# Linear attention plus a routed MLP: eight row numbers loaded at once, and four short runs of the middle stage set in another order

## The chip, the core and the metric

The kernel runs on one core of a Trainium2 chip. The metric is the device time of one execution in microseconds (us), lower is better; times below are in us unless marked ns.

The core's engines work at the same time, each through its own instructions in order, and wait for each other on semaphores: TensorE (PE; PEld are its weight loads) multiplies matrices into PSUM, which has eight banks; VectorE (DVE), ScalarE (ACT) and GpSimd (POOL) work on elements; SyncE (SP) here only issues DMAs.

## The reference, cut

```python
xn = layernorm(x)                                   # x: 2048 x 640, bf16
# A: linear attention, 32 heads of 20
q, k, v = split(xn @ wqkv);  pq, pk = phi(q), phi(k)   # phi(t) = t + 1 or exp(t)
kv, z = pk^T v, sum(pk)                             # per head
A = ((pq kv) / (pq z)) @ wo
# B: eight rows through an MLP
r = xn @ w_r;  idx = the 8 largest of r
y = (silu(xn[idx] @ w_gate) * (xn[idx] @ w_up)) @ w_down * sigmoid(r[idx])
out = x + A + xn + scatter(y at idx)
```

## The kernel before

The 2048 rows are 16 tiles of 128, the 640 columns five chunks of 128. The order on each engine is that of the code (`manual_schedule`); nothing is moved by a scheduler. Semaphore waits are derived from what each instruction reads and writes.

**First stage**, to about 62.8 us: norm, turning (xnT), k, phi(k) into `pk`, q into `pqT`, and G = xn^T pk, which with wv gives kv without v being computed. Columns 0 to 511 of G gather in PSUM banks 0 to 4 (`g_mm`).

**Middle stage**, 62.8 to 82.4 us, where the change lies:

- `grest_mm` (L283) makes G's last 128 columns: 64 matmuls for the first four chunks, 16 for the fifth, all reading `pk`.
- VectorE finds the eight rows (L543 to L560). GpSimd reads the eight numbers one after the other with `value_load` (L565) and copies one column of xnT for each into `xsT` (L566).
- `den_mm` (L581) makes pq z for the first half of the rows, `den_act` (L592, L593) its reciprocal on ScalarE, `spread_mm` (L598) spreads that over the partitions into banks 0 to 3, `spread_copy` (L607) copies it into `spw`, and `scale_by` (L611) multiplies `pqT` by it, a chunk at a time.
- `kv_mm` (L621) makes kv for six groups of heads, `kv_mask` (L633, L640) masks it; `m_mm` (L652) multiplies each group by wo, `m_out` (L664 on ScalarE or L666 on VectorE) copies the result and stores it by SyncE (L667) into M_sb.
- `gu_mm` (L673) makes gate and up from xsT. ScalarE takes Exp, Ln and Exp of gate (L725 to L730, tiles e1 and sg), VectorE two products (L733, L734, tile hm), TensorE turns hm (L741), VectorE copies it (L743, tile hT), and the down product (L749) gives y, which VectorE scales (L756) and GpSimd adds into DRAM (L759); from there x is loaded again (L765).
- `q_mm` (L247) with `q_act` (L259, L260) and `q_phi` (L266) does the remaining q units 13 to 19, a unit being 512 rows of one chunk.

`den_mm`, `gu_mm` and the down product use TensorE as four tiles 32 columns wide, the spread as four tiles of 32 rows; all others use it whole.

Two tiles share memory: `late` is opened under the tag of `pk`, so it has pk's bytes, and whoever writes it waits for pk's readers. M_sb, e1, sg, hm and hT are parts of it:

```python
    late = big.tile([P, T * D], BF16, tag="pk", name="late")
    M_sb = late[:, 0 : KC * D].rearrange("p (k d) -> p k d", k=KC)
    e1 = late[:, o0 : o0 + 2 * FJ].bitcast(F32)
```

**Last stage**, from 82.4 us: per tile of rows ten matmuls pqT x M (L790), VectorE adds x + xn (L800), and the tile is stored. The denominators of the second half run between them.

Of the kernel before, what the change touches and what calls it, by code (L numbers as in the profile page):

```python
# [8 lines left out]
P = 128  # L9
S = 2048  # L10
D = 640
# [3 lines left out]
T = S // P  # L15
# [30 lines left out]
def kernel(  # L46
# [28 lines left out]
    def sb(shape, dt, name, pool=None, tag=None):  # L75
        return (pool or big).tile(shape, dt, tag=tag or name, name=name)
# [34 lines left out]
    candm = sb([P, 2, T, C], BF16, "candm")  # L111
    M_nat5 = sb([GB, D], BF16, "M_nat5")
    spw = sb([P, 2, 4, 256], BF16, "spw")

    ps = psum.tile([P, 8, 512], F32, tag="ps", name="ps")
    xxd = dram.tile([4 * S + P, YW], BF16, tag="xxd", name="xxd")
# [260 lines left out]
    def const_piece(i):  # L377
        if i == 0:
            nc.gpsimd.memset(headg[:], 1.0)
            nc.gpsimd.affine_select(  # L380
                out=headg[:], in_=headg[:], compare_op=ALU.is_ge, fill=0.0, base=0,
                pattern=[[-4, H]], channel_multiplier=1,
            )
            nc.gpsimd.affine_select(
                out=headg[:], in_=headg[:], compare_op=ALU.is_ge, fill=0.0, base=3,
                pattern=[[4, H]], channel_multiplier=-1,
            )
            nc.gpsimd.memset(ones_bf[:], 1.0)
            nc.gpsimd.memset(eps6[:], 1e-6)
            nc.gpsimd.memset(xsT[:], 0.0)  # L390
        elif i == 1:
            nc.gpsimd.memset(maskkv[:], 1.0)
            nc.gpsimd.affine_select(
                out=maskkv[:], in_=maskkv[:], compare_op=ALU.is_ge, fill=0.0, base=0,
                pattern=[[-DH, HG], [0, DH]], channel_multiplier=1,
            )
            nc.gpsimd.affine_select(
                out=maskkv[:], in_=maskkv[:], compare_op=ALU.is_ge, fill=0.0, base=DH - 1,
                pattern=[[DH, HG], [0, DH]], channel_multiplier=-1,
            )  # L400
        elif i == 4:
            nc.gpsimd.memset(ones_r[:], 1.0)
            nc.gpsimd.memset(candm[:], 0.0)
            nc.gpsimd.memset(kvT[:, NG - 1, 0 : W0], 0.0)
            nc.gpsimd.memset(diag[:], 0.0)
            nc.gpsimd.affine_select(
                out=diag[:], in_=diag[:], compare_op=ALU.not_equal, fill=1.0, base=0,
                pattern=[[-1, T]], channel_multiplier=1,
            )
            nc.gpsimd.memset(oh8[:], 0.0)  # L410
            for j in range(4):
                nc.gpsimd.affine_select(
                    out=oh8[:], in_=oh8[:], compare_op=ALU.not_equal, fill=1.0,
                    base=-32 * j, pattern=[[-1, C]], channel_multiplier=1,
                )
        elif i == 5:
            nc.gpsimd.iota(itmp[:], pattern=[[1, P]], base=0, channel_multiplier=0)
            nc.gpsimd.tensor_copy(iot[:], itmp[:])
            nc.gpsimd.iota(
                itmp[:].rearrange("p (t c) -> p t c", c=C), pattern=[[P, T], [0, C]], base=0,  # L420
                channel_multiplier=0,
            )
            nc.gpsimd.tensor_copy(
                tileoff[:], itmp[:].rearrange("p (t c) -> p t c", c=C)
            )
        elif i == 6:
            nc.gpsimd.iota(itmp[:, 0:1], pattern=[[0, 1]], base=4 * S, channel_multiplier=1)
            nc.gpsimd.tensor_copy(yoff[:, 1:2], itmp[:, 0:1])
            nc.gpsimd.memset(yoff[:, 0:1], 0.0)
            for j in range(4):  # L430
                sl = slice(32 * j, 32 * j + C)
                nc.gpsimd.memset(yoff[sl, 0:1], 4.0)
                nc.gpsimd.memset(yoff[sl, 1:2], float(j))
# [97 lines left out]
    )  # L531
    for c in range(KC):
        nc.scalar.copy(GT[:, c, 0:512], ps[:, c, :])
    for t in range(9):
        grest_mm(t, 0, 4, 7)

    allc = sb([P, P], F32, "allc")
    gv = sb([P, C], F32, "gv")
    posu = sb([P, C], U32, "posu")
    junk = sb([P, P], F32, "junk")  # L540
    pcol = sb([P, 4], F32, "pcol")
    idxw = sb([P, 2], U32, "idxw")
    nc.vector.max(gv[:], ps[:, 5, 0:P])  # L543
    nc.vector.max_index(posu[:], gv[:], ps[:, 5, 0:P])
    nc.vector.tensor_tensor(
# [4 lines left out]

    nc.vector.scalar_tensor_tensor(
        out=junk[:, 0:C], in0=posu[:], scalar=1.0, in1=oh8[:], op0=ALU.mult, op1=ALU.mult,
        accum_out=pcol[:, 0:1],
    )
    nc.vector.scalar_tensor_tensor(
        out=junk[:], in0=iot[:], scalar=pcol[:, 0:1], in1=allc[:], op0=ALU.is_equal,
        op1=ALU.mult, accum_out=pcol[:, 1:2],
    )
    nc.vector.tensor_copy(idxw[:, 0:1], pcol[:, 1:2])
    nc.vector.tensor_scalar(  # L560
        out=idxw[:, 1:2], in0=pcol[:, 1:2], scalar1=yoff[:, 0:1], scalar2=yoff[:, 1:2],
        op0=ALU.mult, op1=ALU.add,
    )
    for i in range(C):
        tok = nc.gpsimd.value_load(idxw[i : i + 1, 0:1], min_val=0, max_val=S - 1)  # L565
        nc.gpsimd.tensor_copy(xsT[:, :, i : i + 1], xnT[:, :, bass.ds(tok, 1)])  # L566

    nc.vector.transpose(zT[:], zs[:])
# [8 lines left out]
    def den_mm(h, b):  # L577
        for kc in range(KC):
            for j in range(4):
                o = h * HALF + 256 * j  # L580
                nc.tensor.matmul(  # L581
                    ps[32 * j : 32 * j + 32, b, 0:256],
                    lhsT=zm[:, kc, :],
                    rhs=pqT[:, kc, o : o + 256],
                    start=(kc == 0), stop=(kc == KC - 1),
                    tile_position=(0, 32 * j),
                )
# [15 lines left out]
                tile_position=(32 * j, 0),  # L603
            )

    def spread_copy(h):
        nc.scalar.copy(spw[:, h, :, :], ps[:, 0:4, 0:256])  # L607

    def scale_by(h, m):
        dst = pqT[:, m, h * HALF : (h + 1) * HALF].rearrange("p (j f) -> p j f", j=4)  # L610
        nc.vector.tensor_tensor(out=dst, in0=dst, in1=spw[:, h, :, :], op=ALU.mult)  # L611

    den_mm(0, 6)
    den_act(0, 6)


    def kv_mm(g0, g1, bank):
# [72 lines left out]
    def q_unit(u, b):  # L690
        q_mm(u, b)
        q_act(u, b)
# [7 lines left out]
    with nc.allow_low_precision(reason="gate is bf16 as in the reference"):  # L700
        nc.vector.reciprocal(gbf[:], gcol[:, 2:3])
    nc.vector.tensor_copy(gcol[:, 3:4], gbf[:])
    kv_mm(0, 4, 4)
    kv_mask(0, 4, 4)
    for t in range(9, 11):
        grest_mm(t, 0, 4, 7)
    spread_mm(0)
    spread_copy(0)
    for t in range(11, T):
        grest_mm(t, 0, 4, 7)  # L710
    nc.scalar.copy(GT[:, 0:4, 512:D], ps[:, 7, :].rearrange("p (c f) -> p c f", c=4))
    m_mm(0, 4)
    m_out(0, 4)
    m_mm(1, 0)
    m_out(1, 0, True)
    m_mm(2, 2)
    m_out(2, 2)
    for t in range(T):
        grest_mm(t, 4, 5, 6)
    nc.vector.tensor_copy(GT[:, 4, 512:D], ps[:, 6, 0:P])  # L720
    m_mm(3, 4)
    m_out(3, 4, True)
    scale_by(0, 0)
    gu_mm(wg_sb, 7)
    nc.scalar.activation(e1, ps[:, 7, 0:FJ], AF.Exp, scale=-1.0)  # L725
    gu_mm(wu_sb, 0)
    kv_mm(4, 6, 6)
    scale_by(0, 1)
    nc.scalar.activation(e1, e1, AF.Ln, bias=1.0)
    nc.scalar.activation(sg, e1, AF.Exp, scale=-1.0)  # L730
    kv_mask(4, 5, 6)
    kv_mask5(6)
    nc.vector.tensor_tensor(out=hm, in0=ps[:, 7, 0:FJ], in1=sg, op=ALU.mult)  # L733
    nc.vector.tensor_tensor(out=hm, in0=hm, in1=ps[:, 0, 0:FJ], op=ALU.mult)  # L734
    q_unit(13, 1)
    m_mm(4, 2)
    m_out(4, 2, True)
    m_mm(5, 4)
    m_out(5, 4, True)
    for j in range(3):  # L740
        nc.tensor.transpose(psb(7)[:, j * P : (j + 1) * P], hm[:, j * P : (j + 1) * P], ident[:])  # L741
    q_mm(14, 6, 0, 3)
    nc.vector.tensor_copy(hT, psb(7)[:, 0:FJ].rearrange("p (b c) -> p b c", b=3))  # L743
    q_phi(13)
    scale_by(0, 2)
    for fc in range(FC):
        j, b = fc // 3, fc % 3
        for i in range(4):
            nc.tensor.matmul(  # L749
                ps[32 * i : 32 * i + 32, 0, 0:YW],  # L750
                lhsT=hT[:, b, 32 * j : 32 * j + 32],
                rhs=wd_sb[:, fc, i * YW : (i + 1) * YW],
                start=(fc == 0), stop=(fc == FC - 1),
                tile_position=(0, 32 * i),
            )
    nc.vector.tensor_scalar(  # L756
        out=y_sb[:], in0=ps[:, 0, 0:YW], scalar1=gcol[:, 3:4], scalar2=None, op0=ALU.mult
    )
    nc.gpsimd.indirect_dma_start(  # L759
        xxd[:], bass.IndirectOffsetOnAxis(ap=idxw[:, 1:2], axis=0), y_sb[:], None,  # L760
        compute_op=ALU.add,
    )

    def reload(t0, t1):
        nc.sync.dma_start(x_sb[:, t0:t1, :], xxd_v[:, t0:t1, :])  # L765
# [1 line left out]
    for t0, t1 in ((0, 1), (1, 2), (2, 4), (4, 6), (6, 8)):  # L767
        reload(t0, t1)

    q_mm(14, 6, 3)  # L770
    q_act(14, 6)
    scale_by(0, 3)
    q_phi(14)
    q_unit(15, 2)
    scale_by(0, 4)
    q_phi(15)
    q_unit(16, 3)
    q_phi(16)
    q_unit(17, 1)
    q_phi(17)  # L780
    q_unit(18, 2)
    q_phi(18)
    q_unit(19, 0)
    q_phi(19)


# [81 lines left out]
```

## Time and profile before

| | |
|---|---|
| median of 3 runs | 110.23 us (110.07 to 110.24) |
| the profiled execution's own time | 110.28 us |
| its span, first to last instruction | 108.6 us |
| TensorE busy | 103.9 us, 96% of the span |
| VectorE, ScalarE, GpSimd busy | 82.8, 58.0, 28.9 us |
| granted TensorE clock, mean | 1.000 |

The profile is of one execution. Its timeline rows give the start in us from the span's start, the length, the engine, the source line, the operation, out<-in and a count, and in brackets the engine's idle time before and what ended it. A row that merges several instructions goes from the first's start to the last's end; a matmul's end is modelled and lies after the start of the next, so that the pace of matmuls is read from start to start. POOLq and SPq are the sequencers of GpSimd and SyncE, which load registers and issue DMAs.

### The profile page before, as it was taken

How to read it: one execution, taken by the hardware profiler on the slowest of the kernel's cores; microseconds unless marked ns; L12 is line 12 of the kernel's file. 1: busy time of each engine (PE TensorE's matmuls, PEld its weight loads, DVE VectorE, ACT ScalarE, POOL GpSimd, SP SyncE). 2: the span in 40 equal slices, each digit the busy share in tenths (PEclk: the TensorE clock that was granted, in tenths of full speed). 3: DMA queues.
4: the chain of work that ended last, by engine and by line, in shares of the span. 5: the costliest groups of instructions: out<-in, count | busy, mean ns of one | idle time of the engine just before them, and what ended most of it. 6: DMA issues, size and time to landing. Idle time of an engine off the chain costs nothing.

```text
span 108.6 us, 2418 instructions
## 1 busy us (share of the span) xinstructions
PE 103.9 (96%) x881; PEld 66.0 (61%) x881; DVE 82.8 (76%) x183; ACT 58.0 (53%) x122; POOL 28.9 (27%) x84
## 2 busy tenths in 40 slices
PE   4999999999999999999999999999999999999980
PEld 1376565566555665566556688965656577777760
DVE  0778998989888888988788983558786669966670
ACT  1548846855686558755785574776798330000000
POOL 7402033567744987630000003300420000000000
PEclk9999999999999999999999999999999999999999
DMA  3998961263999999999954799425227928993333
GB/s 97 303 298 265 366 245 25 40 122 60 277 218 191 228 358 189 305 374 300 367 217 166 221 293 374 150 76 157 75 16 203 339 75 231 285 324 132 127 120 114
DMA packets 23096, 22.59 MB, mean 208 GB/s; under 512 B 8796, under 2 KB 21804, under 8 KB 23084
## 3 DMA queue, kind: packets, MB, share of 16 engines
q1 hardware_dynamic: 21106, 20.37, 65.1%
q10 hardware_dynamic: 1834, 2.02, 5.5%
q0 software_dynamic: 144, 0.04, 0.6%
q8 instruction: 7, 0.11, 0.4%
q14 instruction: 5, 0.04, 0.1%
HBM read 14.52 MB, written 5.28 MB: 182 GB/s over the span
## 4 chain that ended last, share of the span: by engine, by line
PE 94%; DVE 2%; POOL 0%; issue 0%; DVEq 0%; POOLq 0%
PE ps L213 20%; PE ps L247 20%; PE ps L790 19%; PE ps L274 16%; PE ps L283 4%; PE ps L294 4%; PE ps L621 2%; PE ps L673 2%; PE ps L195 2%; PE ps L652 2%; DVE xn L800 1%; PE ps L581 1%; PE ps L503 1%; PE ps L749 1%; POOL GT L134 0%; PE ps L598 0%
## 5 line engine op out<-in xcount | busy, mean ns | idle before, releaser
L213 PE MATMUL ps<-wk_sb,xnT 128*128 128x320 bf16 (+1 forms) x160 | 24.6, 300 | 0.2 <-DVE xnT L205 0.2
L247 PE MATMUL ps<-xnT,wq_sb 128*128 128x512 bf16 x100 | 24.2, 379 | 0.0
L790 PE MATMUL ps<-late,pqT 128*128 128x320 bf16 (+2 forms) x165 | 22.3, 295 | 0.0
L213 PEld LDWEIGHTS <-xnT 128*128 128x128 bf16 x160 | 15.3, 98 | 8.4 <-DVE xnT L205 0.5
L274 PE MATMUL ps<-pk,xn 128*128 128x512 bf16 x80 | 19.8, 379 | 0.0
L790 PEld LDWEIGHTS <-pqT 128*128 128x128 bf16 x165 | 15.8, 98 | 6.3 <-issue 0.2
L229 ACT ACTIVATE ek<-ps 128x640 bf16<-128x640 f32 x16 | 11.3, 703 | 15.1 <-PE ps L213 15.1
L800 DVE TENSOR_TENSOR xn<-ps,x_sb 128x640 bf16<-128x640 f32 (+3 forms) x18 | 13.2, 748 | 5.5 <-PE ps L790 5.5
L247 PEld LDWEIGHTS <-wq_sb 128*128 128x128 bf16 x100 | 11.5, 118 | 7.7
L266 DVE SCALAR_TENSOR_TENSOR pqT<-eq,rq 128x512 bf16<-128x512 bf16 x20 | 13.8, 688 | 2.8 <-ACT rq L260 2.8
L236 DVE SCALAR_TENSOR_TENSOR pk<-ek,rk 128x640 bf16<-128x640 bf16 x16 | 12.9, 805 | 1.7 <-ACT rk L230 1.6
L259 ACT ACTIVATE eq<-ps 128x512 bf16<-128x512 f32 x20 | 12.3, 617 | 2.7 <-PE ps L247 2.7
L274 PEld LDWEIGHTS <-xn 128*128 128x128 bf16 x80 | 7.7, 98 | 8.4
L260 ACT ACTIVATE rq<-ps 128x512 bf16<-128x512 f32 x20 | 12.3, 616 | 0.0
L230 ACT ACTIVATE rk<-ps 128x640 bf16<-128x640 f32 x16 | 11.2, 700 | 0.0
L171 POOL TENSOR_TENSOR rs<-mv,half 128x1 f32<-128x1 f32 x13 | 5.8, 449 | 18.1 <-DVE mv L169 18.1
L174 POOL TENSOR_TENSOR rs<-rs,half 128x1 f32<-128x1 f32 x13 | 10.0, 767 | 1.0
L165 DVE BATCH_NORM_STATS2 st<-x_sb 128x6 f32<-128x320 bf16 x16 | 7.6, 478 | 3.2 <-DMA x_sb<-in_A_x_dram 3.2
L183 DVE TENSOR_SCALAR xn<-x_sb,mv,rs 128x640 bf16<-128x640 bf16 x16 | 7.2, 449 | 3.4 <-POOL rs L174 3.3
L168 DVE BATCH_NORM_STATS2 st<-x_sb 128x6 f32<-128x320 bf16 x16 | 7.6, 477 | 0.0
L566 POOL COPY xsT<-xnT 128x5 bf16 x8 | 1.6, 206 | 21.7 <-DVE junk L694 18.3
L189 DVE TENSOR_TENSOR x_sb<-x_sb,xn 128x640 bf16<-128x640 bf16 x16 | 6.9, 476 | 0.0
(123 smaller groups left out, 94.2 us busy)
## 6 DMA issues: line engine op xcount, KB each, us to landing
x_sb<-in_A_x_dram SPq DMA_DIRECT2D x6, 320.0 KB, 8.2
wg_sb<-in_B_w_gate_dram SPq DMA_DIRECT2D x5, 384.0 KB, 4.2
wu_sb<-in_B_w_up_dram SPq DMA_DIRECT2D x5, 384.0 KB, 5.6
wd_sb<-in_B_w_down_dram SPq DMA_DIRECT2D x3, 640.0 KB, 8.3
xxd<-x_sb SPq DMA_DIRECT2D x2, 640.0 KB
out_dram<-xn SPq DMA_DIRECT2D x8, 160.0 KB, 1.8
x_sb<-xxd SPq DMA_DIRECT2D x2, 640.0 KB, 4.9
out_dram<-xn ACTq DMA_DIRECT2D x7, 160.0 KB, 3.2
```

The lines of the kernel that those rows point to most:

```text
L174: nc.gpsimd.tensor_tensor(out=rs[:, 1:2], in0=rs[:, 0:1], in1=half[:, 1:2], op=ALU.pow)
L213: nc.tensor.matmul(ps[:, b + h, 0:w], lhsT=xnT[:, kc, t * P : (t + 1) * P], rhs=wk_sb[:, kc, h * HW : h * HW + w], start=(kc == 0), stop=( ...
L229: nc.scalar.activation(e[:], ps[:, b : b + 2, 0:HW], AF.Exp)
L230: nc.scalar.activation(r[:], ps[:, b : b + 2, 0:HW], AF.Relu)
L236: nc.vector.scalar_tensor_tensor(out=pk[:, t, :].rearrange("p (b f) -> p b f", b=2), in0=e[:], scalar=1.0, in1=r[:], op0=ALU.min, op1=ALU.add,
L247: nc.tensor.matmul(ps[:, b, :], lhsT=wq_sb[:, kc, :].rearrange("p (f m) -> p m f", m=KC)[:, m, :], rhs=xnT[:, kc, tb * TBLK : (tb + 1) * T ...
L259: nc.scalar.activation(e[:], ps[:, b, :], AF.Exp)
L260: nc.scalar.activation(r[:], ps[:, b, :], AF.Relu)
L266: nc.vector.scalar_tensor_tensor(out=pqT[:, m, tb * TBLK : (tb + 1) * TBLK], in0=e[:], scalar=1.0, in1=r[:], op0=ALU.min, op1=ALU.add,)
L274: nc.tensor.matmul(ps[:, c, :], lhsT=xn[:, t, c * P : (c + 1) * P], rhs=pk[:, t, 0:512], start=(t == 0), stop=(t == T - 1),)
L790: nc.tensor.matmul(ps[:, b, 0 : c1 - c0], lhsT=pqT[:, kc, t * P : (t + 1) * P], rhs=M_sb[:, kc, c0:c1], start=(kc == 0), stop=(kc == KC - 1),)
L800: nc.vector.tensor_tensor(out=xn[:, t, c0:c1].rearrange("p (b f) -> p b f", f=w), in0=ps[:, b : b + n, 0:w], in1=x_sb[:, t, c0:c1].rearran ...
```

## The change

**Row numbers.** VectorE gathers the eight numbers in one column of `pcol`, turns that 32x32 block into a row (`prow`), takes the minimum with 2047 into `idxr`, and GpSimd loads all eight registers with one instruction, without a check of bounds for each. The eight copies follow.

**Order of the middle stage.** All 64 matmuls of `grest_mm` for the first four chunks come first, then kv of four groups, then den, gate, up and the spread without others between them, then the 16 of the fifth chunk. q unit 13, M of groups 0 and 1, the turning of hm, kv of the last two groups, M of group 2, the down product, and M of groups 3 to 5 follow, then q units 14 to 19, with a `scale_by` after each `q_phi`. The spread's copy is split: banks 2 and 3 go to VectorE, banks 0 and 1 to ScalarE. Banks are given out anew. No matmul is added or taken away.

```diff
+    pcol = sb([P, 32], F32, "pcol")
...
+            nc.gpsimd.memset(pcol[:], 0.0)
...
-    for t in range(9):
+    for t in range(T):
         grest_mm(t, 0, 4, 7)
...
-    nc.vector.tensor_copy(idxw[:, 0:1], pcol[:, 1:2])
+    nc.vector.transpose(prow[:], pcol[0:32, :])
     nc.vector.tensor_scalar(
+        out=idxr[:], in0=prow[0:1, 0:C], scalar1=float(S - 1), scalar2=None, op0=ALU.min
+    )
...
-    for i in range(C):
-        tok = nc.gpsimd.value_load(idxw[i : i + 1, 0:1], min_val=0, max_val=S - 1)
+    _, toks = nc.values_load_multi_w_load_instructions(
+        idxr[0:1, 0:C], engines=[mybir.EngineType.Pool], min_val=0, max_val=S - 1,
...
+    for i, tok in enumerate(toks):
         nc.gpsimd.tensor_copy(xsT[:, :, i : i + 1], xnT[:, :, bass.ds(tok, 1)])
...
-    den_mm(0, 6)
-    den_act(0, 6)
...
-    kv_mm(0, 4, 4)
-    kv_mask(0, 4, 4)
-    for t in range(9, 11):
-        grest_mm(t, 0, 4, 7)
-    spread_mm(0)
-    spread_copy(0)
-    for t in range(11, T):
-        grest_mm(t, 0, 4, 7)
-    nc.scalar.copy(GT[:, 0:4, 512:D], ps[:, 7, :].rearrange("p (c f) -> p c f", c=4))
-    m_mm(0, 4)
-    m_out(0, 4)
+    kv_mm(0, 4, 5)
+    nc.scalar.copy(GT[:, 0:4, 512:D], ps[:, 7, :].rearrange("p (c f) -> p c f", c=4))
+    kv_mask(0, 4, 5)
+    den_mm(0, 6)
+    den_act(0, 6)
+    gu_mm(wg_sb, 4)
+    nc.scalar.activation(e1, ps[:, 4, 0:FJ], AF.Exp, scale=-1.0)
+    gu_mm(wu_sb, 5)
+    nc.scalar.activation(e1, e1, AF.Ln, bias=1.0)
+    nc.scalar.activation(sg, e1, AF.Exp, scale=-1.0)
+    spread_mm(0)
+    spread_copy(0, 2, 4, False)
+    spread_copy(0, 0, 2)
+    for t in range(T):
+        grest_mm(t, 4, 5, 7)
+    nc.vector.tensor_copy(GT[:, 4, 512:D], ps[:, 7, 0:P])
+    nc.vector.tensor_tensor(out=hm, in0=ps[:, 4, 0:FJ], in1=sg, op=ALU.mult)
+    nc.vector.tensor_tensor(out=hm, in0=hm, in1=ps[:, 5, 0:FJ], op=ALU.mult)
+    q_unit(13, 6)
+    m_mm(0, 2)
+    m_out(0, 2)
     m_mm(1, 0)
     m_out(1, 0, True)
...
+    kv_mm(4, 6, 7)
+    kv_mask(4, 5, 7)
+    kv_mask5(7)
     m_mm(2, 2)
-    m_out(2, 2)
-    for t in range(T):
-        grest_mm(t, 4, 5, 6)
-    nc.vector.tensor_copy(GT[:, 4, 512:D], ps[:, 6, 0:P])
-    m_mm(3, 4)
-    m_out(3, 4, True)
-    scale_by(0, 0)
-    gu_mm(wg_sb, 7)
...
+    m_out(2, 2, True)
...
+    m_mm(3, 0)
+    m_out(3, 0, True)
+    m_mm(4, 2)
+    m_out(4, 2)
+    m_mm(5, 6)
+    m_out(5, 6, True)
+    q_unit(14, 4)
+    q_phi(13)
...
+    scale_by(0, 0)
+    q_unit(15, 5)
+    q_phi(14)
+    scale_by(0, 1)
...
```

ScalarE's instructions in the middle stage before, from the copies of G on (`ld` and `rd` are the reciprocals, `late` the three activations on gate, `M_nat` are groups of M):

```order
L533 CAST GT<-ps 128x512 x5
L592 ACTIVATE ld_1138<-ps,eps_100 128x256
L593 ACTIVATE rd_1139<-ld_1138 128x256
L698 ACTIVATE gcol<-gcol 128x1
L607 CAST spw<-ps 128x1024
L711 CAST GT<-ps 128x4x128
L664 CAST M_nat<-ps 120x640 x2
L725 ACTIVATE late<-ps 128x384
L729 ACTIVATE late<-late 128x384
L730 ACTIVATE late<-late 128x384
```

The same place of the changed kernel, with its own line numbers:

```order
L535 CAST GT<-ps 128x512 x5
L709 ACTIVATE gcol<-gcol 128x1
L715 CAST GT<-ps 128x4x128
L602 ACTIVATE ld_1147<-ps,eps_100 128x256
L603 ACTIVATE rd_1148<-ld_1147 128x256
L720 ACTIVATE late<-ps 128x384
L722 ACTIVATE late<-late 128x384
L723 ACTIVATE late<-late 128x384
L619 CAST spw<-ps 128x512
L260 ACTIVATE eq_1224<-ps 128x512
L261 ACTIVATE rq_1225<-ps 128x512
L675 CAST M_nat<-ps 120x640 x3
```

The three activations on gate stood behind the spread's copy and two groups of M; now they stand ahead of the spread's copy (half as long), of q unit 13 and of all of M.

VectorE behind the mask of the first four groups, before:

```order
L633 TENSOR_TENSOR kvT<-ps,maskkv 120x480
L666 CAST M_nat<-ps 120x640 x2
L720 CAST GT<-ps 128x128
L611 TENSOR_TENSOR pqT<-pqT,spw 128x1024 x2
L633 TENSOR_TENSOR kvT<-ps,maskkv 120x120
L640 TENSOR_TENSOR kvT<-ps,maskkv 120x40
L733 TENSOR_TENSOR late<-ps,late 128x384
L734 TENSOR_TENSOR late<-late,ps 128x384
L743 COPY late<-ps 128x384
```

and in the changed kernel:

```order
L644 TENSOR_TENSOR kvT<-ps,maskkv 120x480
L621 CAST spw<-ps 128x512
L729 CAST GT<-ps 128x128
L730 TENSOR_TENSOR late<-ps,late 128x384
L731 TENSOR_TENSOR late<-late,ps 128x384
L677 CAST M_nat<-ps 120x640
L739 COPY late<-ps 128x384
L644 TENSOR_TENSOR kvT<-ps,maskkv 120x120
L651 TENSOR_TENSOR kvT<-ps,maskkv 120x40
```

The two products of hm moved ahead of every copy of M and of every scaling of pqT, and one copy of M stands between them and the copy of hT.

GpSimd at the row numbers, before, the first two of eight turns (ISA rows compute on registers):

```order
L565 TENSOR_LOAD idxw
L565 ISA x2
L566 ISA
L566 COPY xsT<-xnT 128x5
L565 TENSOR_LOAD idxw
```

and in the changed kernel, the load and the first two of eight copies:

```order
L571 TENSOR_LOAD idxr
L576 ISA
L576 COPY xsT<-xnT 128x5
L576 ISA
L576 COPY xsT<-xnT 128x5
```

One load stands in place of eight, and each turn has one register instruction in place of three and a load.

More of the change, by code (lines that the diff above doesn't have):

```diff
@@ L540 @@
     junk = sb([P, P], F32, "junk")
-    pcol = sb([P, 4], F32, "pcol")
-    idxw = sb([P, 2], U32, "idxw")
+    prow = sb([32, 32], F32, "prow")
+    idxr = sb([1, C], U32, "idxr")
+    idxw = sb([P, 1], U32, "idxw")
     nc.vector.max(gv[:], ps[:, 5, 0:P])
@@ L552 @@
         out=junk[:, 0:C], in0=posu[:], scalar=1.0, in1=oh8[:], op0=ALU.mult, op1=ALU.mult,
-        accum_out=pcol[:, 0:1],
+        accum_out=pcol[:, 1:2],
     )
     nc.vector.scalar_tensor_tensor(
-        out=junk[:], in0=iot[:], scalar=pcol[:, 0:1], in1=allc[:], op0=ALU.is_equal,
-        op1=ALU.mult, accum_out=pcol[:, 1:2],
+        out=junk[:], in0=iot[:], scalar=pcol[:, 1:2], in1=allc[:], op0=ALU.is_equal,
+        op1=ALU.mult, accum_out=pcol[:, 0:1],
     )
-    nc.vector.tensor_copy(idxw[:, 0:1], pcol[:, 1:2])
+    nc.vector.transpose(prow[:], pcol[0:32, :])
     nc.vector.tensor_scalar(
-        out=idxw[:, 1:2], in0=pcol[:, 1:2], scalar1=yoff[:, 0:1], scalar2=yoff[:, 1:2],
+        out=idxr[:], in0=prow[0:1, 0:C], scalar1=float(S - 1), scalar2=None, op0=ALU.min
+    )
+    nc.vector.tensor_scalar(
+        out=idxw[:], in0=pcol[:, 0:1], scalar1=yoff[:, 0:1], scalar2=yoff[:, 1:2],
         op0=ALU.mult, op1=ALU.add,
     )
-    for i in range(C):
-        tok = nc.gpsimd.value_load(idxw[i : i + 1, 0:1], min_val=0, max_val=S - 1)
+    _, toks = nc.values_load_multi_w_load_instructions(
+        idxr[0:1, 0:C], engines=[mybir.EngineType.Pool], min_val=0, max_val=S - 1,
+        skip_runtime_bounds_check_because="each is the minimum of a sum >= 0 and S - 1",
+    )
+    for i, tok in enumerate(toks):
         nc.gpsimd.tensor_copy(xsT[:, :, i : i + 1], xnT[:, :, bass.ds(tok, 1)])
@@ L604, in spread_mm, with spread_copy @@
             )
-    def spread_copy(h):
-        nc.scalar.copy(spw[:, h, :, :], ps[:, 0:4, 0:256])
+    def spread_copy(h, j0=0, j1=4, by_act=True):
+        dst, src = spw[:, h, j0:j1, :], ps[:, j0:j1, 0:256]
+        if by_act:
+            nc.scalar.copy(dst, src)
+        else:
+            nc.vector.tensor_copy(dst, src)
     def scale_by(h, m):
@@ L714 @@
+    nc.vector.tensor_tensor(out=hm, in0=hm, in1=ps[:, 5, 0:FJ], op=ALU.mult)
+    q_unit(13, 6)
+    m_mm(0, 2)
+    m_out(0, 2)
     m_mm(1, 0)
     m_out(1, 0, True)
-    m_mm(2, 2)
-    m_out(2, 2)
-    for t in range(T):
-        grest_mm(t, 4, 5, 6)
-    nc.vector.tensor_copy(GT[:, 4, 512:D], ps[:, 6, 0:P])
-    m_mm(3, 4)
-    m_out(3, 4, True)
-    scale_by(0, 0)
-    gu_mm(wg_sb, 7)
-    nc.scalar.activation(e1, ps[:, 7, 0:FJ], AF.Exp, scale=-1.0)
-    gu_mm(wu_sb, 0)
-    kv_mm(4, 6, 6)
@@ L728 @@
[L728 to L745, printed above, removed]
+    for j in range(3):
+        nc.tensor.transpose(psb(4)[:, j * P : (j + 1) * P], hm[:, j * P : (j + 1) * P], ident[:])
+    nc.vector.tensor_copy(hT, psb(4)[:, 0:FJ].rearrange("p (b c) -> p b c", b=3))
+    kv_mm(4, 6, 7)
+    kv_mask(4, 5, 7)
+    kv_mask5(7)
+    m_mm(2, 2)
+    m_out(2, 2, True)
     for fc in range(FC):
@@ L749 @@
             nc.tensor.matmul(
-                ps[32 * i : 32 * i + 32, 0, 0:YW],
+                ps[32 * i : 32 * i + 32, 5, 0:YW],
                 lhsT=hT[:, b, 32 * j : 32 * j + 32],
@@ L756 @@
     nc.vector.tensor_scalar(
-        out=y_sb[:], in0=ps[:, 0, 0:YW], scalar1=gcol[:, 3:4], scalar2=None, op0=ALU.mult
+        out=y_sb[:], in0=ps[:, 5, 0:YW], scalar1=gcol[:, 3:4], scalar2=None, op0=ALU.mult
     )
     nc.gpsimd.indirect_dma_start(
-        xxd[:], bass.IndirectOffsetOnAxis(ap=idxw[:, 1:2], axis=0), y_sb[:], None,
+        xxd[:], bass.IndirectOffsetOnAxis(ap=idxw[:], axis=0), y_sb[:], None,
         compute_op=ALU.add,
     )
+    m_mm(3, 0)
[6 more added lines that the diff above has]
+    q_phi(13)
     def reload(t0, t1):
@@ L768 @@
         reload(t0, t1)
-    q_mm(14, 6, 3)
-    q_act(14, 6)
+    scale_by(0, 0)
+    q_unit(15, 5)
+    q_phi(14)
+    scale_by(0, 1)
+    q_unit(16, 0)
+    q_phi(15)
+    scale_by(0, 2)
+    q_unit(17, 1)
+    q_phi(16)
     scale_by(0, 3)
-    q_phi(14)
-    q_unit(15, 2)
+    q_unit(18, 2)
+    q_phi(17)
     scale_by(0, 4)
[L776 to L781, printed above, removed]
+    q_unit(19, 3)
     q_phi(18)
-    q_unit(19, 0)
     q_phi(19)
```

## The prediction, as it was put on record

> **What bounds the kernel now.** I read the page's chain of work first, then TensorE's timeline over the stretch that the change rewrites, then the other engines there.
>
> ```profile
> span 108.6 us, 2418 instructions
> PE 94%; DVE 2%; POOL 0%; issue 0%; DVEq 0%; POOLq 0%
> ```
>
> 94% of the chain that ended last is TensorE's own work, so only what shortens, lengthens or interrupts TensorE's stream counts. The stretch on TensorE (start, length of the merged row, line):
>
> ```profile
> 62.79 2.17 PE L283 MATMUL ps<-pk,xn 128*128 128x128 bf16 x36
> 64.94 0.73 PE L581 MATMUL ps<-pqT,zm 128*32 128x256 bf16 x20
> 65.60 1.31 PE L621 MATMUL ps<-GT,wv_sb 128*120 128x120 bf16 x20
> 66.74 0.61 PE L283 MATMUL ps<-pk,xn 128*128 128x128 bf16 x8
> 67.28 0.29 PE L598 MATMUL ps<-rd,gbig 32*128 32x256 bf16 x4
> 67.50 1.29 PE L283 MATMUL ps<-pk,xn 128*128 128x128 bf16 x20
> 68.63 0.98 PE L652 MATMUL ps<-wo_sb,kvT 120*120 120x320 bf16 x6
> 69.45 1.06 PE L283 MATMUL ps<-pk,xn 128*128 128x128 bf16 x16
> 70.34 0.44 PE L652 MATMUL ps<-wo_sb,kvT 120*120 120x320 bf16 x2
> 70.71 1.00 PE L673 MATMUL ps<-wg_sb,xsT 128*32 128x384 bf16 x20
> 71.53 0.99 PE L673 MATMUL ps<-wu_sb,xsT 128*32 128x384 bf16 x20
> 72.45 0.72 PE L621 MATMUL ps<-GT,wv_sb 128*120 128x120 bf16 x10
> 73.02 1.24 PE L247 MATMUL ps<-xnT,wq_sb 128*128 128x512 bf16 x5
> 74.09 0.71 PE L652 MATMUL ps<-wo_sb,kvT 120*120 120x320 bf16 x4
> 74.71 0.34 PE L741 MATMUL ps<-ident,late 128*128 128x128 bf16 x3
> 74.89 0.81 PE L247 MATMUL ps<-xnT,wq_sb 128*128 128x512 bf16 x3
> 75.63 1.01 PE L749 MATMUL ps<-wd_sb,late 128*32 128x160 bf16 x48
> 76.57 6.02 PE L247 MATMUL ps<-xnT,wq_sb 128*128 128x512 bf16 x27
> 82.43 0.30 PE L790 MATMUL ps<-late,pqT 128*128 128x320 bf16 x1
> ```
>
> The starts are what to use: row to row they give the pace. Sixteen L283 take 69.45 to 70.34, 0.056 us each; six L652 0.82, so 0.136 each; five L247 1.08, so 0.215; gate's twenty L673 0.82. Against these paces each row in 32-wide tiles (32 in the 128*32 or 32*128 of its form) is late at both its ends: the eight L283 ahead of the spread take 0.54 where 8 x 0.056 is 0.45 (0.09 going in); up takes 0.92 where gate, with up behind it, takes 0.82 (0.10 coming out); two L652 ahead of gate take 0.37 for 0.27 (0.10, going in). Den's 0.66 and the spread's 0.22 contain 0.10 of coming out.
>
> **The change, part by part.**
>
> *Gain: fewer ways in and out.* Before has four such runs here (den, spread, gate with up, down). After has two: den, gate, up, spread back to back, and down. Two entries and two exits go, about 4 x 0.10, and with them 0.05 that den's entry waited beyond 0.09 (36 L283 take 2.15, not 2.01). One cost may come back, between up (128*32) and spread (32*128): no row shows that boundary. Bounds are 0, as between gate and up, and 0.10, as at every change of form above; I take 0.10. The Trainium skill, "TensorEngine Tiling (Array Packing)", Key Properties, says that changing the tiling mode, though not the tile, drains TensorE. By it this boundary costs and gate to up doesn't, so 0.10; without it the sum below would be 0.10 less. The trace agrees at the boundaries it has.
>
> *A new wait.* Tile late lies in pk's bytes, so whoever writes late waits for pk's last reader, the last L283. Before already shows that wait, on the first M store:
>
> ```profile
> 70.54 7.02 SPq L667 DMA_DIRECT2D late<-M_nat x6
> 69.10 1.56 DVE L666 CAST M_nat<-ps 120x640 bf16<-120x640 f32 x2 [1.17 <-PE ps L652]
> ```
>
> The first of the two copies was done by about 69.9; its store went at 70.54, when the sixteen L283 had ended (69.45 + 1.06 = 70.51). Before runs those ahead of gate. After puts gate, up and spread ahead of them, and gate's Exp, at L725 in before, writes late: so it now waits until the last L283, behind the spread, has ended. ScalarE works in order, and behind that Exp stand Ln, Exp and the spread copy of banks 0 and 1, which m_mm(1) on TensorE needs.
>
> ```profile
> 66.28 0.42 ACT L593 ACTIVATE rd<-ld 128x256 bf16<-128x256 f32 x1
> 66.61 0.19 ACT L698 ACTIVATE gcol<-gcol 128x1 f32<-128x1 f32 x1
> 68.83 0.58 ACT L711 CAST GT<-ps 128x512 bf16<-128x512 f32 x1 [0.20 <-PE ps L283]
> 71.76 0.49 ACT L725 ACTIVATE late<-ps 128x384 f32<-128x384 f32 x1 [0.25 <-PE ps L673]
> 72.28 0.52 ACT L729 ACTIVATE late<-late 128x384 f32<-128x384 f32 x1
> 72.83 0.52 ACT L730 ACTIVATE late<-late 128x384 bf16<-128x384 f32 x1
> 73.52 0.55 DVE L733 TENSOR_TENSOR late<-ps,late 128x384 bf16<-128x384 f32 x1
> 74.10 0.55 DVE L734 TENSOR_TENSOR late<-late,ps 128x384 bf16<-128x384 bf16 x1
> 75.09 0.36 DVE L743 COPY late<-ps 128x384 bf16<-128x384 bf16 x1 [0.44 <-PE ps L741]
> ```
>
> The three activations take 73.35 - 71.76 = 1.59; a copy of 128x512 takes 0.58 and starts about 0.1 before its independent forerunner ends (66.61 against 66.70); the two products take 74.65 - 73.52 = 1.13, and TensorE's transposes started 0.06 after them.
>
> *TensorE's new timetable.* Nothing ahead of 62.79 changes but one POOL memset. 64 L283: 3.58, to 66.37. kv of four groups, 20 x 0.055 (their row less exit): 1.10, to 67.47. Entry 0.09, den 0.56, gate 0.82, up 0.82: to 69.76. Boundary 0.10, spread with exit 0.22: 70.08. Sixteen L283: 70.97. q unit 13: 72.05. m_mm(0): 72.32. Here m_mm(1) is ready and isn't released. The last L283 ends at 70.08 + 1.06 = 71.14, Exp starts about 71.20, sg is done at 72.79, the copy runs 72.70 to 73.28, m_mm(1) starts at 73.34: **a stall of 1.02**. It ends at 73.61. The transposes wait for the products, which start at 72.85 and end at 73.98: start 74.04, **a stall of 0.43**. Then transposes 0.18, kv of the last groups 0.55, m_mm(2) at about 74.80 (m_out(0) on VectorE, 0.82 from about 73.90, ends as it wants the banks) to 75.07, entry 0.09, down 0.95, to 76.11; hT, one 0.36 copy behind m_out(0), is there by 75.1. Then m_mm(3) to (5) 0.82, to 76.93, and thirty L247, 30 x 0.2155 = 6.47: the output product starts at 83.40 instead of 82.43, **0.97 later**. Stalls of 1.45 less 0.48 saved.
>
> *Row numbers.* They must reach xsT before gate at 68.12.
>
> ```profile
> 64.01 0.15 DVE L559 CAST idxw<-pcol 128x1 uint32<-128x1 f32 x1
> 64.27 0.33 DVE L568 STREAM_TRANSPOSE zT<-zs 128x160 bf16<-128x160 bf16 x1
> 65.48 0.21 POOL L566 COPY xsT<-xnT 128x5 bf16 x1 [18.29 <-DVE junk L694]
> 66.20 0.21 POOL L566 COPY xsT<-xnT 128x5 bf16 x1 [0.51 <-issue]
> L565 POOLq TENSOR_LOAD <-idxw x8: 287/288/498, 64.2 to 69.7; - x8
> ```
>
> Before, the first copy starts 1.32 after L559's end (64.16) and the period is 66.20 - 65.48 = 0.72, of which 0.21 is the copy. After replaces L559 by a transpose and a minimum: 0.15 to 0.33 each, so the numbers are there at 64.4 to 64.7, and the first copy goes between 65.5 and 65.9 (one load; its two check instructions are gone). Seven further periods have as bounds 0.21 (copies back to back) and 0.72; without load and check I take 0.26, near the copy, and the last is done at 65.7 + 1.82 + 0.21 = 67.7, 0.4 ahead of gate. From 0.31 a period on gate would wait. A later gate delays Exp and all that follows by as much.
>
> *What else could be late.* VectorE now runs five q_phi and five scalings in turn behind unit 14, at some 0.61 each; the last scaling ends about 84.3 and the output product wants it at 83.40 + 8 x 0.136 = 84.49. A cover of 0.2: nothing, or up to 0.2 more. The output product itself has the same order as before, and y's scatter is issued about 0.7 earlier, which nothing waits for on the chain.
>
> *Sum.* The profiled run took 110.28, 0.05 above the median, of which 108.6 is the span. 110.28 + 0.97 = 111.25; against the median, **111.2**.
>
> **Rivals.**
> 1. *The wait doesn't bite.* If gate's Exp could go as gate ends, ScalarE would be through before m_mm(1), and only about 0.1 of waiting for the products would stay: the output product would start at 81.95, 0.48 earlier, 109.75. For it: the gain at the run's ends is plain in the rows. Against it: the built program's only wait on that Exp is for TensorE's count at the last L283, and L667 shows such a wait.
> 2. *The numbers are late* (slower still). If one load of eight costs eight periods' worth, copies finish as before, by that period near 65.48 + 7 x 0.72 + 0.21 = 70.73, plus 0.3 for the two VectorE steps: gate 2.9 late, 111.2 + 2.9 = 114.1. The 0.51 between copies speaks for it a little (load, checks and address together); that the new load stands once speaks against.
> 3. *Gain and stalls cancel*: 110.2 needs 0.9 less stall, for instance if TensorE's stream up to the last L283 ran ahead of my timetable while ScalarE shortened its 2.2 us to 1.3. No row is that fast.
>
> **How the numbers follow.** Forecast 111.2, chance 0.80: its bounds are the boundary (-0.10), ScalarE's overlaps (-0.3), VectorE's last scaling (+0.2) and a copy period up to 0.35 with a late first copy (+0.5): 110.8 to 111.9. Rival 1: 0.07. Rival 3: 0.05. Rival 2, in part or whole, past 111.9: 0.08. These three lie outside and hold 0.20, so the range is 110.8 to 111.9. Faster by over 0.2% (about what a measurement can tell here, 0.22 us) 0.07, within it 0.05, slower 0.88.
>
> **What would show it.** Right: on TensorE an idle of about 1.0 ahead of the second m_mm, released by ScalarE's spread copy, and 0.4 ahead of the transposes, released by VectorE; gate's Exp starting just behind the sixteen L283. Den to spread without gaps in some 2.6. Wrong: m_mm(1) following m_mm(0) at once (rival 1), or TensorE waiting for xsT ahead of gate (rival 2), or an output product that waits for its fifth slice of pqT.

## The result, and the profile after

The changed kernel took 111.05 us (median; 111.01 to 111.51) against 110.18 for the kernel before in runs on the same chip: a ratio of 1.008, 95% interval 1.0062 to 1.0098. It is slower, by 0.87 us; the forecast was 111.2. The profiled execution took 111.18, its span is 109.5 us.

TensorE's timeline of the changed kernel, from the first `grest_mm` (now L284) to the first matmul of the output product (L798); a bracket is the engine's idle time and what ended it:

```profile
62.74 3.74 PE L284 MATMUL ps<-pk,xn 128*128 128x128 bf16 x64
66.31 1.26 PE L632 MATMUL ps<-GT,wv_sb 128*120 128x120 bf16 x20
67.50 0.73 PE L591 MATMUL ps<-pqT,zm 128*32 128x256 bf16 x20
68.06 0.99 PE L684 MATMUL ps<-wg_sb,xsT 128*32 128x384 bf16 x20
68.87 0.99 PE L684 MATMUL ps<-wu_sb,xsT 128*32 128x384 bf16 x20
69.79 0.29 PE L608 MATMUL ps<-rd,gbig 32*128 32x256 bf16 x4
70.01 1.07 PE L284 MATMUL ps<-pk,xn 128*128 128x128 bf16 x16
70.91 1.24 PE L248 MATMUL ps<-xnT,wq_sb 128*128 128x512 bf16 x5
71.99 0.44 PE L663 MATMUL ps<-wo_sb,kvT 120*120 120x320 bf16 x2
73.24 0.43 PE L663 MATMUL ps<-wo_sb,kvT 120*120 120x320 bf16 x2 [0.81 <-ACT spw L619]
73.95 0.34 PE L738 MATMUL ps<-ident,late 128*128 128x128 bf16 x3 [0.28 <-DVE late L731]
74.13 0.68 PE L632 MATMUL ps<-GT,wv_sb 128*120 128x120 bf16 x10
74.68 0.43 PE L663 MATMUL ps<-wo_sb,kvT 120*120 120x320 bf16 x2
75.04 1.01 PE L748 MATMUL ps<-wd_sb,late 128*32 128x160 bf16 x48
75.98 1.03 PE L663 MATMUL ps<-wo_sb,kvT 120*120 120x320 bf16 x6
76.85 6.64 PE L248 MATMUL ps<-xnT,wq_sb 128*128 128x512 bf16 x30
83.32 0.84 PE L798 MATMUL ps<-late,pqT 128*128 128x320 bf16 x5
```

The two brackets are the two stalls. Read from start to start they are longer than the brackets, since the modelled end of a matmul lies after the next could start: 73.24 - 71.99 less 0.27 for two matmuls is 0.98, and 73.95 - 73.24 - 0.27 is 0.44. The same stretch took 82.43 - 62.79 = 19.64 before and takes 83.32 - 62.74 = 20.58 now: 0.94 more, as much as the spans differ by (109.5 - 108.6 = 0.9). From the output product to the end of the span it was 108.6 - 82.4 = 26.2 and is 109.5 - 83.3 = 26.2.

ScalarE and VectorE at the same place, cut:

```profile
71.11 0.49 ACT L720 ACTIVATE late<-ps 128x384 f32<-128x384 f32 x1 [1.85 <-PE ps L284]
72.19 0.52 ACT L723 ACTIVATE late<-late 128x384 bf16<-128x384 f32 x1
72.62 0.57 ACT L619 CAST spw<-ps 128x512 bf16<-128x512 f32 x1
72.75 0.56 DVE L730 TENSOR_TENSOR late<-ps,late 128x384 bf16<-128x384 f32 x1 [1.27 <-ACT late L723]
73.34 0.55 DVE L731 TENSOR_TENSOR late<-late,ps 128x384 bf16<-128x384 bf16 x1
83.47 0.68 DVE L625 TENSOR_TENSOR pqT<-pqT,spw 128x1024 bf16<-128x1024 bf16 x1
```

ScalarE sits idle for 1.85 while gate's result, complete at about 69.1, lies in its bank, and is released by L284: the last of the sixteen matmuls that read pk. Everything below follows from 71.11: the copy that m_mm(1) wants ends at 73.19, the products at 73.89.

The stretch from the first `grest_mm` to the output product is used below as a second measure beside the medians: between the profiled runs the first `grest_mm` starts anywhere from 62.50 to 63.14, though no kernel changes the matmuls ahead of it, and differences of 0.2 would drown in that.

### The profile page after: what moved, and what is told of

Same layout as the page of the kernel before. It is cut to its first block, busy times and chain, and to the rows that moved or that the text cites. A ratio compares the mean times of both kernels' runs of the same rounds, so it can differ in the third digit from the quotient of the medians.

```text
span 109.5 us, 2400 instructions
## 1 busy us (share of the span) xinstructions
PE 103.7 (95%) x881; PEld 66.1 (60%) x881; DVE 83.5 (76%) x185; ACT 57.4 (52%) x122; POOL 28.2 (26%) x85
## 4 chain that ended last, share of the span: by engine, by line
PE 92%; DVE 3%; ACT 1%; POOL 0%; issue 0%; DVEq 0%; POOLq 0%
PE ps L214 20%; PE ps L798 19%; PE ps L248 19%; PE ps L275 16%; PE ps L284 4%; PE ps L295 4%; PE ps L196 2%; PE ps L684 1%; PE ps L632 1%; DVE xn L808 1%; PE ps L591 1%; PE ps L663 1%; PE ps L505 1%; PE ps L748 1%; DVE late L730 1%; DVE late L731 1%
## 5 line engine op out<-in xcount | busy, mean ns | idle before, releaser
L798 PE MATMUL ps<-late,pqT 128*128 128x320 bf16 (+2 forms) x165 | 22.3, 295 | 0.0
L798 PEld LDWEIGHTS <-pqT 128*128 128x128 bf16 x165 | 15.8, 98 | 6.3 <-issue 0.2
L625 DVE TENSOR_TENSOR pqT<-pqT,spw 128x1024 bf16<-128x1024 bf16 x10 | 6.8, 683 | 0.0
```

Of the source, the lines that this page charges most:

```text
L798: nc.tensor.matmul(ps[:, b, 0 : c1 - c0], lhsT=pqT[:, kc, t * P : (t + 1) * P], rhs=M_sb[:, kc, c0:c1], start=(kc == 0), stop=(kc == KC - 1),)
```

## The experiments

Of the first four runs, e1 to e3 change who waits for what, and e5 prices the way in and out of the narrow tiles. Then e4 and e6 take the two parts of the change apart, and e7 goes on from e1.

**e1: other bytes for the MLP's tiles.**

```diff
-    o0 = KC * D
-    e1 = late[:, o0 : o0 + 2 * FJ].bitcast(F32)
+    mid = big.tile([P, KC * F], BF16, tag="wg_sb", name="mid")
+    o0 = 0
+    e1 = mid[:, o0 : o0 + 2 * FJ].bitcast(F32)
...
```

(sg, hm and hT likewise.)

> The changed kernel with e1, sg, hm and hT laid into the bytes of the gate weights (dead once gate is done) instead of those of pk; nothing else differs. Theory 1, shared bytes: gate's Exp then waits for gate alone and starts near 69.2 instead of 71.1, sg is done near 70.85, m_mm(1) follows m_mm(0) without a gap, the two products end near 72.6 and the transposes wait 0.1 instead of 0.43; both stalls together fall from 1.4 to 0.1, so 1.3 less than the changed kernel: 109.75, 0.4% under before. Theory 2, ScalarE's queue itself is too long there: little changes, 111.0.

Measured: 109.99, ratio to before 0.9983 (0.9965 to 1.0002). In its profile, ScalarE's gate Exp, TensorE around M, and VectorE:

```profile
68.94 0.47 ACT L721 ACTIVATE mid<-ps 128x384 f32<-128x384 f32 x1
70.00 0.52 ACT L724 ACTIVATE mid<-mid 128x384 bf16<-128x384 f32 x1
70.95 0.29 DVE L730 CAST GT<-ps 128x128 bf16<-128x128 f32 x1 [0.34 <-PE ps L284]
71.24 0.56 DVE L731 TENSOR_TENSOR mid<-ps,mid 128x384 bf16<-128x384 f32 x1
62.50 3.74 PE L284 MATMUL ps<-pk,xn 128*128 128x128 bf16 x64
71.76 0.71 PE L663 MATMUL ps<-wo_sb,kvT 120*120 120x320 bf16 x4
72.45 0.34 PE L739 MATMUL ps<-ident,mid 128*128 128x128 bf16 x3
81.82 1.93 PE L799 MATMUL ps<-late,pqT 128*128 128x320 bf16 x13
```

Exp starts at 68.94, just behind gate's end at 68.81 (gate runs from 67.82, with a row of 0.99), and the four matmuls of m_mm(0) and (1) stand in one row. The stretch is 81.82 - 62.50 = 19.32: 1.26 less than the changed kernel and 0.32 less than before. That is theory 1. The median against before shows half of it (0.17%, with an interval that just holds none), so it is the stretch that says how much the order saves without the wait. What is left ahead of the transposes, 72.45 - 71.76 - 4 x 0.136 = 0.15, has a cause of its own: sg was done at 70.52, but VectorE first had to make a copy of G that came from TensorE at 70.95.

**e2: pk's last reader ahead of gate**, bytes shared as in the change.

```diff
+    for t in range(T):
+        grest_mm(t, 4, 5, 4)
+    nc.vector.tensor_copy(GT[:, 4, 512:D], ps[:, 4, 0:P])
     kv_mm(0, 4, 5)
...
-    for t in range(T):
-        grest_mm(t, 4, 5, 7)
-    nc.vector.tensor_copy(GT[:, 4, 512:D], ps[:, 7, 0:P])
```

> The changed kernel with the sixteen matmuls of the fifth chunk moved up behind the other 64, ahead of kv (in bank 4), pk's bytes shared as they were. Theory 1: pk's last reader is gone before gate, so Exp waits for gate alone; gate comes 0.9 later than in e1, Exp starts near 69.95, sg is done near 71.55, the products end near 72.75, the transposes wait 0.25: 1.15 less than the changed kernel, 109.9. Theory 2: 111.0, since ScalarE has the same instructions in the same order.

Measured: 109.97, ratio 0.9977 (0.9964 to 0.999). The ends of the stretch, and gate's Exp:

```profile
62.64 4.63 PE L284 MATMUL ps<-pk,xn 128*128 128x128 bf16 x80
69.97 0.47 ACT L723 ACTIVATE late<-ps 128x384 f32<-128x384 f32 x1
82.17 1.52 PE L798 MATMUL ps<-late,pqT 128*128 128x320 bf16 x10
```

The stretch is 82.17 - 62.64 = 19.53: 1.05 less than the changed kernel, where 1.15 was expected. Exp starts at 69.97, expected near 69.95, behind gate's end at 68.86 + 0.99 = 69.85; the transposes still wait 72.79 - 71.92 - 0.54 = 0.33, for 0.25. ScalarE has the same instructions in the same order as in the change, so its load is not the cause; when pk's last reader runs is.

**e3: the spread's copy off ScalarE.**

```diff
-    spread_copy(0, 2, 4, False)
-    spread_copy(0, 0, 2)
+    spread_copy(0, 0, 4, False)
```

> The changed kernel with the whole copy of the spread on VectorE, so that m_mm(1) waits for nothing of ScalarE. Theory 1: Exp still starts near 71.1 and the products end near 73.9; the first stall (1.0) goes and the second grows by as much, 0.4 to 1.4, so the time stays at 111.05 within 0.1. Theory 2, the copy standing behind the activations is what costs: 1.0 less, 110.05.

Measured: 111.32, ratio 1.0103 (1.0086 to 1.0119); its interval overlaps that of the change, though the median lies 0.27 over it where 0.1 was expected at most. TensorE in its profile:

```profile
62.53 3.74 PE L284 MATMUL ps<-pk,xn 128*128 128x128 bf16 x64
71.78 0.71 PE L663 MATMUL ps<-wo_sb,kvT 120*120 120x320 bf16 x4
73.74 0.34 PE L737 MATMUL ps<-ident,late 128*128 128x128 bf16 x3 [1.25 <-DVE late L730]
83.12 0.57 PE L797 MATMUL ps<-late,pqT 128*128 128x320 bf16 x3
```

The first stall is gone, the second is 73.74 - 71.78 - 0.54 = 1.42 instead of 0.44, and the stretch is 83.12 - 62.53 = 20.59 against 20.58: no gain, and in this stretch no loss. A reader of the profile after who goes by the longest bracket (ScalarE's spread copy) and mends that one gains nothing.

**e5: one more way in and out.** e1 with kv of four groups between den and gate.

```diff
-    kv_mm(0, 4, 5)
+    den_mm(0, 6)
     nc.scalar.copy(GT[:, 0:4, 512:D], ps[:, 7, :].rearrange("p (c f) -> p c f", c=4))
-    kv_mask(0, 4, 5)
-    den_mm(0, 6)
     den_act(0, 6)
+    kv_mm(0, 4, 5)
+    kv_mask(0, 4, 5)
```

> e1 with kv of the first four groups between den and gate instead of ahead of den: one more way out of and into the 32-wide tiles, the same matmuls. Price of one such pair by the rows of before, 0.10 + 0.09 and 0.05 for the first kv matmul: 0.2 more than e1, 109.95. If going in and out costs nothing and the saving came from elsewhere: the same as e1.

Measured: 110.31, ratio 1.0004 (0.9992 to 1.0017), 0.32 over e1. In its profile:

```profile
63.14 3.74 PE L284 MATMUL ps<-pk,xn 128*128 128x128 bf16 x64
66.80 0.73 PE L591 MATMUL ps<-pqT,zm 128*32 128x256 bf16 x20
67.46 1.31 PE L632 MATMUL ps<-GT,wv_sb 128*120 128x120 bf16 x20
82.72 0.98 PE L799 MATMUL ps<-late,pqT 128*128 128x320 bf16 x6
```

The stretch is 82.72 - 63.14 = 19.58, 0.26 over e1's. Den takes 67.46 - 66.80 = 0.66 with its way out, where it took 68.06 - 67.50 = 0.56 in the change with gate right behind it. By the rows, den's way in costs 0.09 behind the 64 (66.80 - 63.14 = 3.66, against 66.31 - 62.74 = 3.57), its way out 0.10, and kv's twenty take 0.05 longer (1.24 against 1.19, each with a way in behind it): 0.24 of the 0.26, where 0.2 was expected. So the prediction's price of about 0.10 for each end holds.

**e4: the old loads in the new order.**

```diff
-    _, toks = nc.values_load_multi_w_load_instructions(
...
-    for i, tok in enumerate(toks):
+    for i in range(C):
+        tok = nc.gpsimd.value_load(idxn[i : i + 1, 0:1], min_val=0, max_val=S - 1)
```

(idxn is a plain copy of the column; the transpose and the minimum are gone.)

> The changed kernel with the row numbers read one after the other as before; order, banks and bytes as in the change. If the new loads are what lets gate stand so early: the eighth column reaches xsT near 70.5, as in before, gate starts near 70.6 instead of 68.06, and everything behind it, the wait on the last L284 included, comes 2.5 later: 113.55. If xsT is in time anyway: 111.05.

Measured: 115.38, ratio 1.0466 (1.0444 to 1.0488). TensorE's rows, and behind them the stretch of gate and up as a row of the view by windows (start:end, length, then busy time of PE, PEld, DVE, ACT and POOL, granted clock, DMA share, GB/s):

```profile
67.45 0.73 PE L583 MATMUL ps<-pqT,zm 128*32 128x256 bf16 x20
70.52 1.73 PE L676 MATMUL ps<-wg_sb,xsT 128*32 128x384 bf16 x20 [2.33 <-POOL xsT L568]
70.52:73.78 3.26, 3.26 (x40) 1.48 (x41) 0.00 (x0) 0.00 (x0) 0.00 (x0) 0.52 0.00 0
```

The wait came as expected: gate starts 70.52 - 67.45 - 0.56 = 2.51 late. But the kernel lost 4.33 to the changed one, not 2.5. Gate and up took 73.78 - 70.52 = 3.26 instead of 69.79 - 68.06 = 1.73, at a granted clock of 0.52: 1.53 more, right behind the wait. The spread behind them took 74.11 - 73.78 = 0.33 instead of 0.22. The three add up to 4.15, which is what the stretch grew by (87.42 - 62.69 = 24.73 against 20.58); the medians of the two runs give 0.2 more. So the new order leans on the new loads: with the old ones it is far slower than before.

**e6: the new loads in the old order.** The diff is the part of the change on row numbers alone.

> The kernel before with the row numbers turned and loaded at once, and nothing else of the change. TensorE reaches gate at 70.7 in before by its own stream, whose last L652 ends there; the entry of 0.1 falls on gate in any case. Theory: xsT is done near 66.8 and nobody wants it before 70.6: 110.2, no change within 0.1. Rival, the loads had held gate back: up to 0.1 faster, as much as the gap ahead of gate.

Measured: 110.32, ratio 1.0016 (1.0003 to 1.003): at most slightly slower, where both theories said the same or faster. The interval only just leaves out no change; the rows say more. VectorE and TensorE in its profile:

```profile
63.82 0.20 DVE L562 STREAM_TRANSPOSE prow<-pcol 32x32 f32<-32x32 f32 x1
64.06 0.16 DVE L563 TENSOR_SCALAR idxr<-prow 1x8 uint32<-1x8 f32 x1
64.68 0.24 DVE L578 TENSOR_TENSOR zm<-zT,headg 128x160 bf16<-128x160 bf16 x1
62.60 2.17 PE L284 MATMUL ps<-pk,xn 128*128 128x128 bf16 x36
64.97 0.73 PE L590 MATMUL ps<-pqT,zm 128*32 128x256 bf16 x20 [0.20 <-DVE zm L578]
82.47 1.25 PE L799 MATMUL ps<-late,pqT 128*128 128x320 bf16 x8
```

I had asked who waits for xsT and not who else stands behind the two new steps on VectorE: zm does, and den waits for zm. Den starts 64.97 - 62.60 = 2.37 behind the first `grest_mm`, 2.15 before; the stretch is 82.47 - 62.60 = 19.87, 0.23 over before's 19.64. Before, zm ended at 64.64 + 0.24 = 64.88 and den started at 64.94, so the 0.05 that the prediction found ahead of den was this wait too. In the change den stands at 67.50 and the same 0.2 are hidden.

**e7: e1 with the last copy of G on ScalarE**, for the 0.15 that e1 left.

```diff
-    nc.vector.tensor_copy(GT[:, 4, 512:D], ps[:, 7, 0:P])
+    nc.scalar.copy(GT[:, 4, 512:D], ps[:, 7, 0:P])
```

> e1 with the copy of G's last piece (GT, chunk 4) on ScalarE, which sits idle then, instead of on VectorE ahead of the two products. In e1 that copy (0.29 at 70.95) holds the first product back to 71.24, though sg was done at 70.52, and TensorE waits 0.14 ahead of the transposes. Theory: the products end before TensorE wants them, the 0.14 goes, and with it that much of the time: TensorE's stretch from the first L284 to the output product falls from 19.32 to 19.18, 109.85. Rival: q unit 13's activations on ScalarE come later by that copy and M of group 1 with them, nothing gained.

Measured: 109.76, ratio 0.9961 (0.9944 to 0.9978): faster than both kernels. In its profile:

```profile
62.59 3.74 PE L284 MATMUL ps<-pk,xn 128*128 128x128 bf16 x64
71.85 0.71 PE L663 MATMUL ps<-wo_sb,kvT 120*120 120x320 bf16 x4
72.39 0.33 PE L739 MATMUL ps<-ident,mid 128*128 128x128 bf16 x3
72.56 0.68 PE L632 MATMUL ps<-GT,wv_sb 128*120 128x120 bf16 x10
73.20 0.43 PE L663 MATMUL ps<-wo_sb,kvT 120*120 120x320 bf16 x2
81.84 1.93 PE L799 MATMUL ps<-late,pqT 128*128 128x320 bf16 x13
```

The transposes follow m_mm(1) without a gap (72.39 - 71.85 = 0.54 for four). About half of what that gives is lost again one step on: kv's ten take 73.20 - 72.56 = 0.64, not 0.55, ahead of m_mm(2), which needs the banks of m_mm(0), and VectorE copies those from 72.32 to 73.14. The stretch is 81.84 - 62.59 = 19.25, where 19.18 was expected, and 0.39 under before.

## Why the prediction was right, point by point

- **Fewer ways in and out, 0.48 saved.** Measured: 20.58 less the stalls of 0.98 and 0.44 is 19.16, 0.48 under before's 19.64, so the timetable's total holds. But the paragraph on the gain adds up to less, 4 x 0.10 + 0.05 - 0.10 = 0.35. By the rows, 0.34 is the ways in and out that it names: into the spread 0.09, into gate 0.10, out of den 0.10, and the 0.05 ahead of den. The rest is 0.04 that kv lost behind den in before (65.60 to 66.74, 1.14 for 1.10), 0.07 that before's transposes waited for the two products (four L652 take 74.09 to 74.71, 0.62 for 0.55), and some 0.03 of small differences. The timetable had these without a word on them. e5 shows the mechanism and prices one pair.
- **The boundary between up and spread, taken at 0.10.** Up takes 69.79 - 68.87 = 0.92 with the spread behind it, gate 68.87 - 68.06 = 0.81 with up behind it. The value taken holds. So does the rule that the prediction took from the Trainium skill, "TensorEngine Tiling (Array Packing)", Key Properties, as far as time can show it: the change of mode from up to spread costs, the step from gate to up does not.
- **The new wait, 1.02 and 0.43.** Measured 0.98 and 0.44, released by the two named. e1 and e2 take its cause away in two ways and the stretch falls by 1.26 and 1.05; e3 shows that both stalls are one wait. Rival 3 needed 0.9 less of them.
- **The timetable.** Expected 0.97 later at the output product, measured 0.94. Counted from the first `grest_mm`, single steps were off by up to 0.08 (m_mm(3) came 13.24 behind it for 13.32), partly against each other: the wait ahead of m_mm(1) was 0.04 shorter, while the six matmuls of M behind the down product took 0.87 for 0.82, with a loss behind a narrow run that the timetable had left out.
- **Row numbers in time.** In time, but by 1.3, not 0.4, and a bound failed:

```profile
L571 POOLq TENSOR_LOAD <-idxr x1: 760/760/760, 64.4 to 64.4; - x1
65.68 1.09 POOL L576 COPY xsT<-xnT 128x5 bf16 x8 [18.52 <-DVE gcol L710]
```

  One load of eight took 0.76 (0.50 for the first single one before), and all eight copies 1.09, to 66.77. By their 0.21 each I had bounded the period at 0.21 from below; it was (1.09 - 0.21) / 7 = 0.13. With 1.3 to spare that error cost the forecast nothing. Rival 2's lateness was not there; e4 shows what it would have cost, and that 114.1 would have been too low, since the clock wasn't in it.
- **The last scaling.** It ended at 83.47 + 0.68 = 84.15 and was wanted at 83.32 + 8 x 0.136 = 84.41: covered, by about 0.26.
- **What hides the two new VectorE steps** was not said in the prediction for den. It cost nothing in the change, and 0.23 in e6.

## What to carry to other kernels

Before a result is written earlier, look whose bytes it is written into: two tiles under one tag make the writer wait for the other's last reader, wherever that stands on its engine (here it even stood behind the writer in the code), and an in-order engine hands that wait on to everything behind. Two stalls one behind the other can have one cause; mend the cause, as the second grows by what the first loses. Runs of narrow TensorE tiles are worth joining (about 0.25 here for one way in and out) if what feeds them is early enough.

## What the runs showed of the hardware

- **Behind an idle of 2.33 us TensorE's clock was halved.** In e4 gate and up ran at a granted clock of 0.52 right behind the wait and took 1.53 longer than in the change. The mean clock of all four executions of e4 is 0.981 to 0.985, against 0.995 to 1.000 in every other run here, so it came each time. The change's longest idle in this stretch, 0.81 by its bracket, cost no clock (this row is its window from 72.00 to 77.00, columns as above), and neither did e3's of 1.25 (granted clock 1.00 from 73.74 to 77.10):

```profile
72.00:77.00 5.00, 3.91 (x75) 3.02 (x74) 2.99 (x8) 3.91 (x8) 0.20 (x1) 1.00 0.11 32
```

  The Trainium skill, "TensorE: Matmul & The Clock Gate", Why this matters for your kernels, advises against idle gaps over about 3 us; in e4 one of 2.33 was enough. Where between 1.25 and 2.33 the limit lies here is open.
- **Eight small GpSimd copies overlapped, by their rows:** 0.21 each, 1.09 for all eight, so that they started 0.13 apart.
- **The stage ahead of the change moved by 0.6 us between profiled runs** (first `grest_mm` at 62.50 in e1, 63.14 in e5). The cause is open.
